# Reordering the first gate matmuls of a fused state-space and feed-forward kernel: four tiles first, then two double-width tiles, with the fourth token tile loaded earlier

## Chip, cores, metric

The kernel runs on one core of a Trainium2 chip. The metric is the time of one execution in device microseconds (us). "Before" is the kernel without the change, "after" the kernel with it. All runs told here were with a granted TensorE clock of 0.999 or 1.0 of full speed.

Engine names in the profile: PE is TensorE matmul, PEld its weight load, DVE is VectorE, ACT is ScalarE, POOL is GpSimd; SPq and ACTq are the two queues from which this kernel issues its loads. A load "lands" when its data have arrived; the trace records the landing of each load in shares, 16 for a load that fills 128 partitions. "Evicting" is copying a result out of PSUM, the memory into which TensorE writes; PSUM has banks, and this kernel evicts a bank before it uses it again.

## The reference, cut to what matters

```python
def reference(A_x, ...):                 # x is 1 x 2048 x 512
    xn = layernorm(x)                    # per token, over 512 features
    # A: diagonal complex state-space layer, 512 states, scanned over 2048 tokens
    # B: (silu(xn @ w_gate) * (xn @ w_up)) @ w_down, hidden width 1376
    return x + A(xn, ...) + B(xn, w_gate, w_up, w_down)
```

Everything needs `xn`, so nothing useful can run on TensorE before the first tokens are loaded, normalised and transposed. The change is about that start.

## The kernel before

The tokens come in four chunks of 512. TensorE does, for each chunk, gate, up and state-input matmuls, then one long accumulation of the down-projection and the state output. For chunk 0 the gate matmuls of the first six hidden tiles are cut into quarters of 128 tokens (`q`), so that they can start when one tile of 128 tokens is ready. Six PSUM banks stay open for them. In front of the gates PE also runs some matmuls on a constant whose result is not used (`pe_warm`, line 450).

The loads of the start, in the order of their queues (`dma` issues on SP, `act_load` on ACT):

```python
act_q = [pload("ld_ldt", 2, A_log_dt)]                       # a parameter row
dma("ld_x0", ...); dma("ld_x1", ...)                         # 128 tokens each, 128 KB
act_load("ld_wgA0", wg[:, 0:2, 0:FQ], ..., [("wg", "a0")])   # gate tiles 0-3, first half of the contraction
dma("ld_x2", ...)
act_load("ld_wgA1", wg[:, 2:4, 0:FQ], ..., [("wg", "a1")])   # gate tiles 0-3, second half
dma("ld_wg0", wg[:, :, FQ:FH0], ...)                         # gate tiles 4, 5
dma("ld_x3", ...)
act_q.append(pload("ld_lim", ...)); act_q.append(pload("ld_lre", ...))   # parameter rows
```

Normalisation of the first tiles (`bn_st`, `bn_ag` statistics, `ln_ve` variance plus epsilon, `ln_rstd` the power on POOL, `ln_apply` the result) and the gate loop:

```python
def ln_chunk0():
    bn_st(0); bn_ag(0)
    last = ln_ve(0, 1)
    ln_rstd(0, 1)
    last = ln_apply(0, parts=2, order=(bn_st(1, order=(last,)),))
    last = ln_ve(1, 1, order=(bn_ag(1, order=(last,)),))
    ln_rstd(1, 1)
    return bn_st(2, order=(last,))
# ... ln_chunk0_rest(): apply 1; then tiles 2 and 3, with the parameter copy params_ev between

xt_tile_fine(0, parts=2, ...)          # PE transposes of token tile 0, ACT evicts them into xnT
for q in range(4):                     # 128 tokens each
    for ii, (i, bk) in enumerate(tiles):   # six gate tiles
        if q == 0 and ii == 2:
            params_t(...)              # PE transposes the parameter rows
            ln_chunk0_rest(...)
        if q < 3 and ii == (4 if q == 0 else 2):
            xt_tile_fine(q + 1)        # transposes of the next token tile
        # 4 matmuls: wg[:, kt, i] (128 x 128) times xnT[:, 0, q, kt, :] (128 tokens)
```

PE and SP keep the program order written here. The order on DVE, ACT and POOL comes from a list scheduler in the kernel, which works with estimated times.

## Time and profile before

| | before |
|---|---|
| median (runs) at the time of the prediction | 181.9 us (3; 181.77 to 181.97) |
| profiled run | 182.01 us, span 180.3 us |
| PE busy | 97% of the span |
| first gate matmul | 6.76 us |
| first up-projection | 13.47 us |
| last output addition | 177.83 us |

First, two lines of the profile's page (the span, then busy us, share and number of instructions by engine).

```profile
span 180.3 us, 2342 instructions
...
PE 175.3 (97%) x900; PEld 84.9 (47%) x908; DVE 160.8 (89%) x274; ACT 84.5 (47%) x107; POOL 13.5 (7%) x23
...
```

The list of waits of PE (who waited for whom: us in total, times, longest).

```profile
...
PE pb L749 <- ACT xnT L549: 1.0, 2, 0.8
PE pb L450 <- PEq L977: 0.8, 1, 0.8
PE pb L543 <- DVE xn_sb L485: 0.2, 1, 0.2
```

PE waited for 2.0 us in all, always at the start. The chain of work that ended last, in order of time (start, its length in us, what), shows where the end is decided:

```profile
...
6.13 0.63 issue
6.76 0.61 PE pb L749 x8
...
13.63 13.81 PE pb L710 x64
...
177.83 0.42 DVE x_sb L881
```

From 13.63 us on the chain is PE work alone to within 0.05 us at each hand-over, up to the last output addition at 177.83. A gain must come from before 13.5 us, or the tail. The timeline of PE there (start, us, engine, line, operation, output<-inputs, form, count, idle before):

```profile
...
6.76 0.61 PE L749 MATMUL pb<-xnT,wg 128*128 128x128 bf16 x8 [0.75 <-ACT xnT L549]
7.30 0.22 PE L457 MATMUL pb<-ident,prow 4*128 4x4 bf16 x3
7.46 0.62 PE L749 MATMUL pb<-xnT,wg 128*128 128x128 bf16 x8
7.92 0.39 PE L543 MATMUL pb<-ident,xn_sb 128*128 128x128 bf16 x4
8.14 0.61 PE L749 MATMUL pb<-xnT,wg 128*128 128x128 bf16 x8
8.99 0.62 PE L749 MATMUL pb<-xnT,wg 128*128 128x128 bf16 x8 [0.24 <-ACT xnT L549]
...
13.47 0.81 PE L710 MATMUL pb<-xnT,wu 128*128 128x512 bf16 x3
```

How to read it: matmuls of 128 columns start 0.056 us apart but each record lasts 0.22 us, so a group's record ends later than its issue slots. The eight that begin at 8.14 have used their slots by 8.14 + 8 x 0.056 = 8.59. The next group begins at 8.99. The gap is 0.40 us of issue although the line says 0.24. The transposes of token tile 1 (7.92, line 543) are what it waits for: transposes, eviction by ACT and hand-over take 8.99 - 7.92 = 1.07 us.

In the second chain line, "issue" for 0.63 us before 6.76 hides a wait. The timeline names ACT for it, but by the chain ACT had evicted tile 0 by 6.13: the second half of the gate weights was issued at 1.83 us, and the trace's landing records have 15 of its 16 shares by 5.64 us and the last at 6.67. The Trainium skill ("DMA: Bandwidth & Descriptors", section "Why a DMA increments its semaphore by 16 and not by 1") says that only the full 16 means that all data landed. The trace agrees: the first gate matmul starts 0.09 us after the sixteenth.

### The profile page before, as it was taken

What the parts mean: (1) busy time and instruction counts of PE and PEld (TensorE: products, weight loads), DVE (VectorE), ACT (ScalarE), POOL (GpSimd) and SP (SyncE); (2) the same over time, 40 slices, a digit from 0 to 9 for tenths busy, and PEclk for the clock granted to TensorE, in tenths of its full rate; (3) what the DMA queues carried; (4) which work ended last, traced back from release to release, by engine and by line L of the source; (5) the groups of instructions that cost most, each with busy time, mean ns of one, the idle gap of its engine ahead of it and who ended that gap; (6) DMA issues with size and microseconds to landing.
All of it is one profiled execution on the core that took longest, in us unless ns stands there. A gap on an engine that the chain in (4) does not pass through costs nothing.

```text
span 180.3 us, 2342 instructions
## 1 busy us (share of the span) xinstructions
PE 175.3 (97%) x900; PEld 84.9 (47%) x908; DVE 160.8 (89%) x274; ACT 84.5 (47%) x107; POOL 13.5 (7%) x23
## 2 busy tenths in 40 slices
PE   8799999999999999999999999999999999999994
PEld 2494444444444444444444544444444444444643
DVE  3888849989799999979999999999999999999733
ACT  3279899995897991060655653000455620000000
POOL 3251200004200000320000000000000000000000
PEclk9999999999999999999999999999999999999999
DMA  6995556669160000001430000001200000000202
GB/s 163 316 373 127 119 100 104 149 201 343 33 116 0 4 0 0 0 0 61 91 86 0 0 0 4 0 0 36 80 0 4 0 0 0 0 0 33 87 29 87
DMA packets 23410, 12.37 MB, mean 69 GB/s; under 512 B 15112, under 2 KB 23400, under 8 KB 23400
## 3 DMA queue, kind: packets, MB, share of 16 engines
q1 hardware_dynamic: 22832, 11.70, 24.4%
q10 hardware_dynamic: 568, 0.53, 1.0%
q8 instruction: 7, 0.11, 0.3%
q14 instruction: 3, 0.02, 0.0%
HBM read 6.46 MB, written 2.10 MB: 47 GB/s over the span
## 4 chain that ended last, share of the span: by engine, by line
PE 94%; DMA 1%; DVE 1%; issue 1%; ACT 1%; POOL 0%
PE pb L710 39%; PE pb L863 21%; PE pb L781 15%; PE pb L876 15%; PE pb L749 3%; DMA x_sb<-in_A_x_dram 1%; ACT xnT L549 1%; PE pb L543 1%; DVE st L466 0%; POOL rstd L478 0%; DVE x_sb L881 0%; DVE xn_sb L485 0%; DVE mv L470 0%; DVE ve L474 0%; PE pb L457 0%
## 5 line engine op out<-in xcount | busy, mean ns | idle before, releaser
L710 PE MATMUL pb<-xnT,wu 128*128 128x512 bf16 (+1 forms) x176 | 41.2, 379 | 0.0
L821 DVE TENSOR_TENSOR_SCAN rot<-sm,car,rot 128x512 bf16<-128x512 f32 x32 | 38.9, 1267 | 0.0
L863 PE MATMUL pb<-wd,hT 128*128 128x512 bf16 (+3 forms) x183 | 38.0, 366 | 0.2
L710 PE MATMUL pb<-xnT,wg 128*128 128x512 bf16 (+1 forms) x152 | 35.9, 379 | 0.0
L722 ACT ACTIVATE sg<-pb 128x1024 bf16<-128x1024 f32 (+1 forms) x24 | 22.4, 948 | 28.4 <-PE pb L710 28.1
L876 PE MATMUL pb<-W,hss 128*128 128x512 bf16 (+1 forms) x132 | 28.1, 366 | 0.2
L781 PE MATMUL pb<-xnT,BT 128*128 128x512 bf16 x128 | 28.1, 379 | 0.0
L863 PEld LDWEIGHTS pb<-wd,hT 128*128 128x128 bf16 (+1 forms) x187 | 18.3, 98 | 20.0
L768 ACT ACTIVATE uf<-pb 128x1024 bf16<-128x1024 f32 (+1 forms) x24 | 22.7, 950 | 9.4 <-PE pb L710 8.6
L710 PEld LDWEIGHTS pb<-xnT,wu 128*128 128x128 bf16 (+1 forms) x176 | 17.6, 100 | 20.1
L710 PEld LDWEIGHTS pb<-xnT,wg 128*128 128x128 bf16 (+1 forms) x152 | 15.3, 100 | 17.6
L876 PEld LDWEIGHTS pb<-W,hss 128*128 128x128 bf16 x136 | 13.3, 98 | 14.4
L781 PEld LDWEIGHTS pb<-xnT,BT 128*128 128x128 bf16 x128 | 12.5, 98 | 15.0
L788 ACT ACTIVATE u_sb<-pb 128x1024 bf16<-128x1024 f32 x16 | 16.3, 1022 | 5.1 <-PE pb L781 4.8
L770 DVE TENSOR_TENSOR hT<-sg,uf 128x1024 bf16<-128x1024 bf16 (+1 forms) x24 | 14.9, 635 | 2.8 <-ACT uf L768 2.8
L881 DVE TENSOR_TENSOR x_sb<-pb,x_sb 128x512 bf16<-128x512 f32 (+1 forms) x17 | 10.9, 654 | 5.4 <-PE pb L876 5.4
L466 DVE BATCH_NORM_STATS2 st<-x_sb 128x6 f32<-128x512 bf16 x16 | 10.2, 682 | 4.0 <-DMA x_sb<-in_A_x_dram 4.0
L495 ACT ACTIVATE xn_sb<-x_sb,nmr,rstd 128x512 bf16<-128x512 bf16 x8 | 5.9, 802 | 10.5 <-DVE nmr L492 10.5
L812 DVE TENSOR_TENSOR rot<-u_sb,cosT 128x2048 bf16<-128x2048 bf16 x8 | 9.7, 1215 | 0.4 <-ACT u_sb L788 0.4
L812 DVE TENSOR_TENSOR rot<-rot,sin 128x2048 bf16<-128x2048 bf16 x8 | 9.8, 1220 | 0.0
L812 DVE TENSOR_TENSOR rot<-rot,cosT 128x2048 bf16<-128x2048 bf16 x8 | 9.8, 1220 | 0.0
L812 DVE TENSOR_TENSOR rot<-u_sb,sin 128x2048 bf16<-128x2048 bf16 x8 | 9.7, 1214 | 0.0
(62 smaller groups left out, 115.7 us busy)
## 6 DMA issues: line engine op xcount, KB each, us to landing
out_dram<-x_sb SPq DMA_DIRECT2D x15, 128.0 KB, 1.7
x_sb<-in_A_x_dram SPq DMA_DIRECT2D x3, 512.0 KB, 7.6
wd<-in_B_w_down_dram SPq DMA_DIRECT2D x1, 1280.0 KB, 7.0
wu<-in_B_w_up_dram SPq DMA_DIRECT2D x1, 768.0 KB, 6.4
wg<-in_B_w_gate_dram SPq DMA_DIRECT2D x1, 608.0 KB, 7.5
wu<-in_B_w_up_dram SPq DMA_DIRECT2D x1, 608.0 KB, 8.7
x_sb<-in_A_x_dram SPq DMA_DIRECT2D x4, 128.0 KB, 2.8
wg<-in_B_w_gate_dram ACTq DMA_DIRECT2D x2, 256.0 KB, 4.0
```

The lines of the kernel that those rows point to most:

```text
L466: return g.add("dve", lambda e, a=a: e.bn_stats(out=st[:, a, :], in_=x_sb[:, a, :]), reads=[("x", a)], writes=[("st", a)], name="bnst%d" % ...
L710: inst = e.matmul(pbank[0:fs, bk, :].rearrange("p (j t) -> p j t", j=4), lhsT=w[:, kt, i * 128:i * 128 + fs], rhs=xnT[:, c % 2, :, kt, :], ...
L722: g.add("act", lambda e: e.activation(out=sg[rows, sl, 0:n, :].rearrange("p a t -> p (a t)"), in_=pair_f32(rows, bk, 512 * n), func=AF.Sil ...
L768: g.add("act", lambda e: e.activation(out=uf[rows, ul, 0:n, :].rearrange("p a t -> p (a t)"), in_=pair_f32(rows, bk, 512 * n), func=AF.Ide ...
L770: g.add("dve", lambda e: e.tensor_tensor(out=hT[rows, hb, i0:i0 + n, :], in0=sg[rows, sl, 0:n, :], in1=uf[rows, ul, 0:n, :], op=ALU.mult), ...
L781: inst = e.matmul(pbank[:, bk, :].rearrange("p (j t) -> p j t", j=4), lhsT=BT[:, ri, kt, pt * 128:(pt + 1) * 128], rhs=xnT[:, c % 2, :, kt ...
L788: g.add("act", lambda e: e.activation(out=u_sb[:, us].rearrange("p r t -> p (r t)"), in_=pair_f32(slice(0, 128), b0), func=AF.Identity), r ...
L812: tt = lambda out, a, b, op, r, w, nm: g.add("dve", lambda e: e.tensor_tensor(out=out, in0=a, in1=b, op=op), reads=r, writes=w, name="%s_% ...
L821: g.add("dve", lambda e, A0=A0, A1=A1, k=k, ri=ri, pt=pt: e.tensor_tensor_scan(out=A1[:, k, ri, :], data0=rr[:, pt:pt + 1].to_broadcast([1 ...
L863: inst = e.matmul(pbank[:, bk, 0:nc_], lhsT=hT[0:fs, hb, i, lt * 128:(lt + 1) * 128], rhs=wd[0:fs, i, c0:c0 + nc_], start=(i == 0), stop=F ...
L876: inst = e.matmul(pbank[:, bk, 0:nc_], lhsT=hss[:, hb, pt, ri, lt * 128:(lt + 1) * 128], rhs=W12[:, ri, pt, c0:c0 + nc_], start=False, sto ...
L881: g.add("dve", lambda e, bk=bk, a=a, c0=c0, nc_=nc_: e.tensor_tensor(out=x_sb[:, a, c0:c0 + nc_], in0=pbank[:, bk, 0:nc_], in1=x_sb[:, a, ...
```

## The change

The intent: ask for fewer weights early, get the transposes of the second token tile out sooner, and have the tokens' statistics ready in time.

- PE: four gate tiles for tokens 0-127 and then for 128-255; the last two gate tiles later, for both at once (256 columns); transposes of token tile 1 after two gate tiles instead of four.
- Loads: x3 before the weights of gate tiles 4 and 5.
- DVE and POOL: the mean and variance of token tile 1 before tile 0 is applied; tile 1's `ve` on POOL; statistics of tile 3 before the parameter copy.

```diff
+        dma("ld_x3", x_sb[:, 3:4, :], x_v[:, 3:4, :], [("x", 3)], TILEB)
         dma("ld_wg0", wg[:, :, FQ:FH0], wg_v[:, :, FQ:FH0], [("wg", 0)], 512 * (FH0 - FQ) * 2)
-        dma("ld_x3", x_sb[:, 3:4, :], x_v[:, 3:4, :], [("x", 3)], TILEB)
@@ ln_chunk0
-            last = ln_apply(0, parts=2, order=(bn_st(1, order=(last,)),))
-            last = ln_ve(1, 1, order=(bn_ag(1, order=(last,)),))
+            last = bn_ag(1, order=(bn_st(1, order=(last,)),))
+            ln_ve(1, 1, eng="pool")
             ln_rstd(1, 1)
+            last = ln_apply(0, parts=2, order=(last,))
             return bn_st(2, order=(last,))
@@ ln_chunk0_rest
                 if a == 2:
-                    last = params_ev(par_bank, (last,))
-                last = ln_apply(a, order=(bn_st(a + 1, order=(last,)),) if a < 3 else (last,))
+                    last = params_ev(par_bank, (bn_st(3, order=(last,)),))
+                last = ln_apply(a, order=(last,))
@@ ffn_gate_quarters (the loop over q is replaced; gate() is four matmuls, cut here)
+            gate(i, bk, 0, 1, 0, 2, fine=True)      # tile, bank, first quarter, quarters
+            gate(i, bk, 0, 1, 2, 4, fine=True)
+            gate(*tiles[1], 0, 1)
+            params_t(tiles[-1][1])
+            ln_chunk0_rest(last, tiles[-1][1])
+            xt_tile_fine(1)
+            gate(*tiles[2], 0, 1)
+            gate(*tiles[3], 0, 1)
+            gate(*tiles[0], 1, 1)
+            gate(*tiles[1], 1, 1)
+            xt_tile_fine(2)
+            gate(*tiles[2], 1, 1)
+            gate(*tiles[3], 1, 1)
+            gate(*tiles[4], 0, 2)
+            gate(*tiles[5], 0, 2)
+            for ii, t in enumerate(tiles):
+                if ii == 2:
+                    xt_tile_fine(3)
+                gate(*t, 2, 1)
+            for t in tiles:
+                gate(*t, 3, 1)
```

More of the change, by code (lines that the diff above doesn't have):

```diff
@@ L738, in ffn_gate_quarters, with gate, mm @@
             tiles = [(2 * ip + k, banks[ip] + k) for ip in pairs for k in range(2)]
-            for q in range(4):
-                for ii, (i, bk) in enumerate(tiles):
-                    if q == 0 and ii == 2:
-                        params_t(tiles[-1][1])
-                        ln_chunk0_rest(last, tiles[-1][1])
-                    if q < 3 and ii == (4 if q == 0 else 2):
-                        xt_tile_fine(q + 1)
-                    for k0, k1 in (((0, 2), (2, 4)) if q == 0 and ii == 0 else ((0, 4),)):
-                        def mm(e, bk=bk, i=i, q=q, k0=k0, k1=k1):
-                            for kt in range(k0, k1):
-                                inst = e.matmul(pbank[:, bk, q * 128:(q + 1) * 128], lhsT=wg[:, kt, i * 128:(i + 1) * 128], rhs=xnT[:, 0, q, kt, :],
-                                                start=(kt == 0), stop=(kt == KT - 1))
-                            return inst
-                        xr = [("xnT", 0, q)] if q else [("xnT0", h) for h in range((k1 + 1) // 2)]
-                        g.add("pe", mm, reads=wres("wg", i) + xr, writes=BK(bk), name="mm_gq%d_%d" % (i, q), est=(k1 - k0) * 56, ninst=k1 - k0)
+            def gate(i, bk, q0, nq, k0=0, k1=KT, fine=False):
+                def mm(e):
+                    for kt in range(k0, k1):
+                        o = pbank[:, bk, q0 * 128:(q0 + nq) * 128]
+                        inst = e.matmul(o.rearrange("p (j t) -> p j t", j=nq), lhsT=wg[:, kt, i * 128:(i + 1) * 128], rhs=xnT[:, 0, q0:q0 + nq, kt, :],
+                                        start=(kt == 0), stop=(kt == KT - 1))
+                    return inst
+                xr = [("xnT0", h) for h in range((k1 + 1) // 2)] if fine else [("xnT", 0, q0 + j) for j in range(nq)]
+                g.add("pe", mm, reads=wres("wg", i) + xr, writes=BK(bk), name="mm_gq%d_%d" % (i, q0), est=(k1 - k0) * (56 if nq == 1 else 110), ninst=k1 - k0)
@@ new lines, in ffn_gate_quarters @@
+            (i, bk) = tiles[0]
+            gate(i, bk, 0, 1, 0, 2, fine=True)
[11 more added lines that the diff above has]
+            gate(*tiles[3], 1, 1)
```

## The prediction

> **What bounds the kernel now.** TensorE: the busy table gives PE 97% of the 180.3 us span at full granted clock. The chain of waits is PE work without a break from 13.63 us (first up-projection) to 177.8; the list of waits shows PE waiting three times, 0.8, 1.0 and 0.2 us in total, all before 9 us. VectorE is 89% busy but ahead: the last `hss` is ready at 165.9 us and first used at 170.7. So the change can gain only before 13.5 us.
>
> **The first 13.5 us, from the timeline.** Token tile 0 is normalised, transposed and evicted by 6.13 us. The first gate matmul starts at 6.76, and not for the normalisation: the second gate-weight half (ACT queue, issued 1.83) lands at 6.67. Its landing records show 15 of 16 shares by 5.64 us and one at 6.67. The Trainium skill ("DMA: Bandwidth & Descriptors", why a DMA increments its semaphore by 16) says that only all 16 mean landed; the trace agrees. The parameter rows, behind it on that queue, land at 7.06; their transposes start at 7.30. From 6.76 to 13.47 are 6.71 us: 96 gate matmuls x 0.056 = 5.35, 12 transposes x 0.055 = 0.66, parameters 0.16, and about 0.4 idle before 8.99, where PE waits for tile 1's eviction: its transposes start at 7.92, its gates can start 1.07 us later, and only 8 matmuls (0.45 us) stand between. After that no wait.
>
> **What the change does.**
> - PE order: tile 1's transposes come 0.46 us earlier, but its gates follow 8 matmuls behind, as before: 1.07 us against 0.22 + 0.45 of work. The idle of 0.4 us moves to about 8.1-8.5 us and stays. Later evictions remain covered.
> - Eight 256-wide matmuls replace sixteen 128-wide. The Trainium skill ("TensorE: Matmul & The Clock Gate", "Wait — 56ns, not 53.3ns?") gives N / 2.4 GHz plus about 2.5 ns; the trace agrees (56 ns at 128, 216 at 512). Estimate: 0.02 us gained.
> - VectorE: tile 1's mean goes first (tile 0 maybe 0.05 us later), its `ve` moves to POOL, tile 3's statistics precede the parameter copy. Tiles 1 to 3 are ready slightly earlier, but they are ready 0.6-1 us before PE asks, before and after. Off the critical path.
> - x3 (landed 7.57) goes ahead of the weights of gate tiles 4, 5, which are now asked for near 9.7 instead of 8.14; they landed at 7.25, so no wait there before either.
> - Scheduling: a sine table moves ahead of the SiLU evictions (0.65 us); banks have about 1.5 us of slack there.
>
> Sum: first gate start unchanged, gates end at 13.42 instead of 13.47: nominally -0.05 us.
>
> **What can move it.** The straggling weight share and the parameter rows: another DMA (128 packets rather than 512) is now issued just behind. If the straggler goes, gates start at 6.2 and the parameters near 6.7: up to 0.6 us gained. If the larger packets slow it, 0.2-0.3 lost.
>
> **Predicted time: 181.75 us, 80% range 181.3 to 182.15.** Faster by over 2%: 0.005; within 2%: 0.99; slower by over 2%: 0.005.
>
> **What would show it.** Right: first gate matmul at 6.2-6.9 us, at the weights' landing; one PE wait of about 0.4 us for tile 1's eviction, now before 8.5 us; first up-projection at 12.9-13.6 us; PE unbroken from there, so that the total moves by just that start. Wrong: a PE wait for tile 2, 3, gate tiles 4, 5 or a bank; the total moved without the first up-projection; a gap after 13.5 us.

## The result

| | before | after |
|---|---|---|
| median of 6 runs | 181.76 us (181.53 to 181.97) | 181.83 us (181.71 to 182.53) |
| ratio after / before | | 1.0011, 95% interval 0.9993 to 1.0028 |
| profiled run | 182.01 us | 182.53 us |
| second gate-weight half complete | 6.67 us | 6.61 us |
| first gate matmul | 6.76 us | 6.70 us |
| first up-projection | 13.47 us | 13.38 us |
| last output addition | 177.83 us | 178.34 us |

A ratio here is the mean time of one kernel's fast runs over that of the other's of the same rounds, so it is not quite the ratio of the medians in the table. The slowest run after, 182.53, is the one that was profiled; without it the ratio of the means would be 1.0005. The page after:

```profile
span 180.8 us, 2337 instructions
...
PE 175.8 (97%) x900; PEld 84.7 (47%) x900; DVE 160.4 (89%) x273; ACT 84.1 (47%) x107; POOL 14.0 (8%) x24
...
```

The list of waits of PE after, and its timeline of the start:

```profile
...
PE pb L450 <- PEq L995: 0.8, 1, 0.8
PE pb L544 <- DVE xn_sb L485: 0.6, 1, 0.6
PE pb L744 <- DMA wg<-in_B_w_gate_dram: 0.4, 1, 0.4
PE pb L711 <- ACT sg L723: 0.4, 1, 0.4
PE pb L744 <- ACT xnT L550: 0.2, 1, 0.2
```

```profile
...
6.70 0.61 PE L744 MATMUL pb<-xnT,wg 128*128 128x128 bf16 x8 [0.45 <-DMA wg<-in_B_w_gate_dram]
7.23 0.22 PE L457 MATMUL pb<-ident,prow 4*128 4x4 bf16 x3
7.39 0.40 PE L544 MATMUL pb<-ident,xn_sb 128*128 128x128 bf16 x4
7.62 0.61 PE L744 MATMUL pb<-xnT,wg 128*128 128x128 bf16 x8
8.47 0.62 PE L744 MATMUL pb<-xnT,wg 128*128 128x128 bf16 x8 [0.24 <-ACT xnT L550]
...
13.38 1.24 PE L711 MATMUL pb<-xnT,wu 128*128 128x512 bf16 x5
```

The start is as predicted, nearly figure by figure. The first gate matmul follows the landing of its weights, and now the profile names that DMA. Transposes of tile 1 begin 0.16 us after the parameter transposes (7.39 after 7.23) instead of 0.62 (7.92 after 7.30). But the gates that need them begin at 8.47, again 1.08 us later, and again only eight matmuls lie between: 7.62 + 8 x 0.056 = 8.07, so PE issues nothing for 0.40 us. The gap moved and kept its size. First gate matmul to first up-projection is 13.38 - 6.70 = 6.68 us, against 6.71 before.

One thing was not predicted: the fourth wait of the list, `PE pb L711 <- ACT sg L723`, far behind the start. The chain after has it:

```profile
...
1.81 4.80 DMA wg<-in_B_w_gate_dram
6.61 0.09 issue
6.70 0.61 PE pb L744 x8
...
13.54 13.81 PE pb L711 x64
...
51.00 0.92 ACT sg L723
...
178.34 0.42 DVE x_sb L899
```

The timeline at 48 to 53 us, before and then after:

```profile
...
49.35 1.00 ACT L722 ACTIVATE sg<-pb 128x1024 bf16<-128x1024 f32 x1
...
51.45 1.89 PE L710 MATMUL pb<-xnT,wg 128*128 128x512 bf16 x8
...
```

```profile
...
48.06 2.93 ACT L495 ACTIVATE xn_sb<-x_sb,nmr,rstd 128x512 bf16<-128x512 bf16 x4 [2.38 <-DVE nmr L492]
...
50.90 1.00 ACT L723 ACTIVATE sg<-pb 128x1024 bf16<-128x1024 f32 x1
...
51.96 1.25 PE L711 MATMUL pb<-xnT,wg 128*128 128x512 bf16 x5 [0.43 <-ACT sg L723]
...
```

In the run after, ACT began to normalise chunk 2 (line 495, four instructions) at 48.06, because its statistics waited for x tiles 8 to 11. The SiLU eviction (`sg`) stood behind in ACT's order, started 1.55 us later than before (50.90 against 49.35), and PE waited for its bank: 51.96 against 51.45, although PE had been 0.09 us ahead. That costs 0.6 us in this run. The landing records show a cause up the line: one share of the transposing load of `C_re` came at 34.38 us, 1.54 us after the fifteenth, and the DMAs behind it were issued later (x tiles 8 to 11 at 38.30 instead of 36.56 us). Was this part of the change, or an accident of one run? The repeat below decides.

### The profile page after: what moved, and what is told of

It reads as the page before. It is cut to its first block, busy times and chain, and to the rows that moved or that the text cites. A ratio compares the mean times of both kernels' runs of the same rounds, so it can differ in the third digit from the quotient of the medians.

```text
span 180.8 us, 2337 instructions
## 1 busy us (share of the span) xinstructions
PE 175.8 (97%) x900; PEld 84.7 (47%) x900; DVE 160.4 (89%) x273; ACT 84.1 (47%) x107; POOL 14.0 (8%) x24
## 4 chain that ended last, share of the span: by engine, by line
PE 94%; DMA 3%; ACT 1%; ACTq 1%; DVE 0%; issue 0%
PE pb L711 39%; PE pb L881 21%; PE pb L894 15%; PE pb L799 15%; PE pb L744 3%; DMA wg<-in_B_w_gate_dram 3%; ACTq L385 1%; ACT sg L723 1%; PE pb L544 0%; ACT xnT L550 0%; DVE x_sb L899 0%; PE pb L457 0%
## 5 line engine op out<-in xcount | busy, mean ns | idle before, releaser
L711 PE MATMUL pb<-xnT,wu 128*128 128x512 bf16 (+1 forms) x176 | 41.2, 379 | 0.0
L881 PE MATMUL pb<-wd,hT 128*128 128x512 bf16 (+3 forms) x187 | 38.7, 366 | 0.0
L711 PE MATMUL pb<-xnT,wg 128*128 128x512 bf16 (+1 forms) x152 | 35.9, 379 | 0.4 <-ACT sg L723 0.4
L723 ACT ACTIVATE sg<-pb 128x1024 bf16<-128x1024 f32 (+1 forms) x24 | 22.4, 949 | 26.7 <-PE pb L711 26.5
L711 PEld LDWEIGHTS pb<-xnT,wu 128*128 128x128 bf16 (+1 forms) x176 | 17.6, 100 | 20.1
L711 PEld LDWEIGHTS pb<-xnT,wg 128*128 128x128 bf16 (+1 forms) x152 | 15.2, 101 | 18.3 <-ACT sg L723 0.9
L894 PEld LDWEIGHTS pb<-W,hss 128*128 128x128 bf16 x136 | 13.3, 98 | 14.4
```

The source lines that it names most:

```text
L711: inst = e.matmul(pbank[0:fs, bk, :].rearrange("p (j t) -> p j t", j=4), lhsT=w[:, kt, i * 128:i * 128 + fs], rhs=xnT[:, c % 2, :, kt, :], ...
L723: g.add("act", lambda e: e.activation(out=sg[rows, sl, 0:n, :].rearrange("p a t -> p (a t)"), in_=pair_f32(rows, bk, 512 * n), func=AF.Sil ...
L881: inst = e.matmul(pbank[:, bk, 0:nc_], lhsT=hT[0:fs, hb, i, lt * 128:(lt + 1) * 128], rhs=wd[0:fs, i, c0:c0 + nc_], start=(i == 0), stop=F ...
L894: inst = e.matmul(pbank[:, bk, 0:nc_], lhsT=hss[:, hb, pt, ri, lt * 128:(lt + 1) * 128], rhs=W12[:, ri, pt, c0:c0 + nc_], start=False, sto ...
```

## The experiments

Twelve kernels were run, in four groups (e1 to p3, e2 to e5, f1 to f3, and f4 alone, in the order of the table); each group shared its chip and its runs of the kernel before. All were correct.

| kernel | median us (runs) | before in the same rounds | ratio, 95% interval |
|---|---|---|---|
| e1: the change again | 181.89 (5) | 181.85 (11) | 1.0004, 0.9993 to 1.0016 |
| p1: loads only | 181.77 (6) | 181.85 (11) | 0.9998, 0.9986 to 1.0011 |
| p2: normalisation only | 181.94 (5) | 181.85 (11) | 0.9999, 0.9986 to 1.0012 |
| p3: PE order only | 181.94 (5) | 181.85 (11) | 1.0001, 0.9989 to 1.0013 |
| e2: transposes early, six gate tiles | 181.68 (6) | 181.70 (11) | 1.0000, 0.9984 to 1.0017 |
| e3: weights issued first | 181.92 (6) | 181.70 (11) | 1.0012, 0.9997 to 1.0027 |
| e4: e2 and e3 | 181.81 (6) | 181.70 (11) | 1.0006, 0.9992 to 1.0021 |
| e5: e4 with the change's normalisation | 181.78 (6) | 181.70 (11) | 1.0004, 0.9988 to 1.0020 |
| f1: e2 with ACT order mended | 181.46 (6) | 181.85 (11) | 0.9992, 0.9967 to 1.0017 |
| f2: gate weights cut by columns | 182.26 (6) | 181.85 (11) | 1.0017, 0.9997 to 1.0038 |
| f3: f1, f2 and later parameters | 181.49 (6) | 181.85 (11) | 0.9981, 0.9963 to 0.9999 |
| f4: f1 with x 8-11 loaded earlier | 181.36 (6) | 181.75 (11) | 0.9980, 0.9962 to 0.9999 |

And what the profiled run of each shows of the start (us):

| kernel | second gate-weight load complete | first gate matmul | first up-projection | last output addition | profiled run |
|---|---|---|---|---|---|
| before | 6.67 | 6.76 | 13.47 | 177.83 | 182.01 |
| after | 6.61 | 6.70 | 13.38 | 178.34 | 182.53 |
| e1 | 6.45 | 6.54 | 13.36 | 177.72 | 181.89 |
| p1 | 6.09 | 6.18 | 12.95 | 177.31 | 181.48 |
| p2 | 6.82 | 6.95 | 13.66 | 178.01 | 182.18 |
| p3 | 6.80 | 6.89 | 13.58 | 177.94 | 182.12 |
| e2 | 6.44 | 6.53 | 13.39 | 177.75 | 181.95 |
| e3 | 5.88 | 6.45 | 13.34 | 177.69 | 181.87 |
| e4 | 5.34 | 6.55 | 13.42 | 177.78 | 181.94 |
| e5 | 5.23 | 6.68 | 13.06 | 177.41 | 181.59 |
| f1 | 6.09 | 6.39 | 12.74 | 177.10 | 181.29 |
| f2 | 6.97 | 5.93 | 13.55 | 177.91 | 182.09 |
| f3 | 7.00 | 6.00 | 12.83 | 177.19 | 181.36 |
| f4 | 6.04 | 6.13 | 12.52 | 176.88 | 181.06 |

Two readings of this table carry the rest. First, in 13 of the 14 profiles the last output addition comes 164.35 or 164.36 us after the first up-projection; only the run after, with its late wait, has 164.96. So apart from such an accident the total is the start plus a constant: the profiled run's time less its first up-projection is 168.52 to 168.56 us in those 13. Second, wherever the gate weights came last (before, after, p1, p2, p3, f4), the first gate matmul starts 0.09 to 0.13 us after their last share. In e1 and e2 it also starts 0.09 us after, but there the `pe_warm` matmuls in front of it on PE end within 0.02 us of the same moment, so these two cannot tell which was last. The weights' last share moved between 6.04 and 6.82 us over these profiles without a cause in the code that these runs show. The 44 timed runs of the kernel before in the four groups reach from 181.27 to 182.47 us. The start has one more part that moves. In e1, e2 and f1 the last `pe_warm` matmuls (256 columns) started 0.213 us apart, against 0.109 to 0.113 in before and after, and the trace's first record of the full TensorE clock is at 6.82, 6.61 and 6.50 us, against 4.49 and 4.18. In f1 the last of them started at 6.18 and the first gate matmul followed at 6.39, 0.30 us after the weights: PE's own work held it there. **One profile therefore cannot judge a change of half a microsecond here**: p1's profiled run is 0.5 us shorter than that of before, but its six timed runs give a ratio of 0.9998.

### e1: the change, again

No edit.

> The changed kernel unaltered, once more, to see which of its features repeat. Theory (start bound by the second gate-weight half, idle moved and not filled): ratio to the kernel before 0.998 to 1.002; first gate matmul within 0.1 us of the landing of that weight half; a PE wait of about 0.25 us in the list (0.4 us in issue) for tile 1's eviction before 9 us. The PE wait of 0.4 us near 51 us in the first profile of the changed kernel (ACT held by the late normalisation of chunk 2): the accident theory says that it came from one late share of a transpose of the C matrix and is absent or under 0.2 us here; the rival (the change's own order on VectorE and ACT makes it) says that it is here again with 0.4 us or more.

Measured: ratio 1.0004 and no wait of PE after the start:

```profile
...
PE pb L450 <- PEq L995: 0.8, 1, 0.8
PE pb L744 <- ACT xnT L550: 0.2, 1, 0.2
```

The gap is there again (8.46 after 7.61 + 0.45 = 8.06). The wait near 51 us is not, with the same order of instructions on every engine. So that order does not make it by itself. With the late load it did: 1.55 us of delay in the run after, where the kernel before has about 1.1 us to spare. The change's total was the start's in e1, as predicted. From first gate matmul to first up-projection e1 took 6.82 us, not 6.68: its first three steps from one gate matmul to the next took 0.094 to 0.106 us, until the clock record of 6.82, and the rest of the eight 0.055 to 0.057.

### p1, p2, p3: each part alone

p1 swaps the two loads alone, p2 takes the normalisation hunks alone, p3 the PE hunk alone, each on the kernel before, as in the diff of the change.

> The kernel before with only x3 loaded ahead of the weights of gate tiles 4 and 5. Theory: statistics of tile 3 start near 6.9 instead of 7.6 us, nothing on PE moves: first up-projection 13.3 to 13.6 us, ratio 0.998 to 1.002. In this order the weights of tiles 4 and 5 land near 7.9 us and PE asks for them near 8.1, so a wait of up to 0.2 us is possible. Rival (the loads are what the change is worth): ratio under 0.998.

> The kernel before with only the normalisation order of the change (tile 1 mean first, its variance on POOL, tile 3 statistics before the parameter copy). Theory: tile 1 is normalised about 0.1 us earlier, PE asks for it only near 7.9 us, so ratio 0.998 to 1.002 and the first up-projection at 13.3 to 13.6 us. Rival (it delays tile 0 and so the start): first gate matmul later by 0.1 to 0.25 us and ratio 1.001 or more.

> The kernel before with only the PE order of the change (transposes of tile 1 after two gate tiles; gate tiles 4 and 5 late and 256 wide). Theory: the PE gap before the gates of tokens 128-255 moves to about 8.1-8.5 us and stays 0.4 us in issue; first up-projection 13.3 to 13.5 us; ratio 0.998 to 1.002. Rival (the order does fill the gap and something else gives it back): gap under 0.15 us.

Measured: 0.9998, 0.9999 and 1.0001. No part is worth anything that these runs can show; the intervals leave room for 0.14%, or 0.25 us, so larger gains and losses that cancel are excluded. p3 has its tile 1 transposes at 7.59, its two gate tiles from 7.82 and the next gates at 8.68; 8.68 - (7.82 + 0.45) = 0.41 us, the moved gap:

```profile
...
7.82 0.61 PE L743 MATMUL pb<-xnT,wg 128*128 128x128 bf16 x8
8.68 0.62 PE L743 MATMUL pb<-xnT,wg 128*128 128x128 bf16 x8 [0.24 <-ACT xnT L549]
...
```

The rival of p3 (the order fills the gap) falls. In p1 and p2 the starts differ from before by more than the theory allows (first up-projections 12.95 and 13.66 against the 13.3 to 13.6 that I wrote), but by the landing of the second weight half, 6.09 and 6.82; from the first gate matmul to the first up-projection they take 6.77 and 6.71 us. p2's rival said that the start would be late because tile 0 is late; tile 0's transposes end early enough there (second group starts at 5.50), and PE's wait is for the weights.

### e2: fill the gap

On the kernel before:

```diff
-                    if q < 3 and ii == (4 if q == 0 else 2):
+                    if q < 3 and ii == 2:
```

> The kernel before with one edit: the transposes of tile 1 come after two gate tiles as in the change, but the gates of tokens 0-127 keep all six tiles, so 16 matmuls (0.9 us) and not 8 (0.45 us) stand between these transposes and the gates that need them. Theory (too little work behind the transposes is the gap): no PE gap before the gates of tokens 128-255, first up-projection at 13.0 to 13.15 us, ratio 0.9970 to 0.9985 (0.3 to 0.5 us). Rival (start-up gaps are not on the critical path, or something later gives it back): ratio 0.999 or more.

Measured: 1.0000, and 13.39 instead of 13.0 to 13.15. This expectation failed. PE's timeline and, in the second fence, ACT's:

```profile
...
7.55 1.50 PE L749 MATMUL pb<-xnT,wg 128*128 128x128 bf16 x24
...
10.68 1.06 PE L749 MATMUL pb<-xnT,wg 128*128 128x128 bf16 x16
12.04 1.51 PE L749 MATMUL pb<-xnT,wg 128*128 128x128 bf16 x24 [0.31 <-ACT xnT L549]
...
```

```profile
...
10.78 0.73 ACT L660 ACTIVATE scrC<-iot,sm 128x512 f32<-128x512 f32 x1 [0.87 <-DVE sm L612]
11.42 0.57 ACT L549 ACTIVATE xnT<-pb 128x512 bf16<-128x512 bf16 x1
...
```

The first gap is gone: 24 matmuls run without a break from 7.55. But a new gap opens at the last quarter: 10.68 + 16 x 0.056 = 11.58, and the next group begins at 12.04. ACT shows why. The eviction of token tile 3 (line 549) starts at 11.42, although its transposes were issued at 10.45; a sine-table activation (line 660) that was scheduled in front of it ran from 10.78. Before, PE was slower to get there, and the same order cost nothing. What the early transposes had won, 0.40 us, was given back as 0.46 us at the end of the same stage.

### e3, e4, e5: issue the weights earlier

e3, on the kernel before, puts the parameter row behind the weights on the ACT queue:

```diff
-        act_q = [pload("ld_ldt", 2, A_log_dt)]
+        act_q = []
...
         act_load("ld_wgA1", ...)
+        act_q.append(pload("ld_ldt", 2, A_log_dt, (act_q[-1],)))
```

(`act_load` takes `tuple(act_q[-1:])` as its order, since the list may now be empty.) e4 has the edits of e2 and e3, e5 adds the normalisation hunks of the change.

> The kernel before with one edit: on the ACT queue the two gate-weight halves are issued ahead of the parameter row ld_ldt, so about 0.56 us earlier. Theory (the first gate matmul waits for the second half): it starts at 6.15 to 6.35 us, now bound by tile 0's eviction; first up-projection at 12.95 to 13.2 us; ratio 0.9965 to 0.9985. Rival (the landing is set by shared DMA bandwidth or the straggling share and not by the issue): first gate matmul at 6.6 us or later and ratio 0.999 or more. If x0 lands later for it, up to 0.2 us of the gain goes.

> The edits of e2 and e3 together. Theory: gains add, first up-projection at 12.6 to 12.8 us, ratio 0.994 to 0.9965 (0.6 to 1.0 us). Less if tile 1 (normalised by about 6.7 us in the kernel before) or the weights of gate tiles 4 and 5 (landing 7.25) become what PE waits for: then a PE wait for one of them shows, and the gain is 0.4 to 0.6 us.

> e4 with the normalisation order of the change added. Theory: with the start 0.5 us earlier, tile 1's readiness has little slack left, so this order is worth 0 to 0.1 us now; ratio within 0.001 of that of e4. Rival (tile 0 is delayed by tile 1's mean, and tile 0's eviction now sets the start): 0.05 to 0.25 us slower than e4.

Measured: 1.0012, 1.0006 and 1.0004. No gain: e3 and e4 both missed their ranges, and e5 came within 0.001 of e4, as expected. The weights did land earlier (5.88, 5.34, 5.23), but no longer set the start. PE's first groups in e3 (transposes of tile 0, then the gates):

```profile
...
5.71 0.27 PE L544 MATMUL pb<-ident,xn_sb 128*128 128x128 bf16 x2 [0.46 <-DVE xn_sb L486]
...
6.45 0.79 PE L750 MATMUL pb<-xnT,wg 128*128 128x128 bf16 x8
...
```

x0 landed at 3.41 instead of 2.93 us, x1 at 4.46 instead of 3.67. Tile 0's transposes began at 5.71 instead of 5.14, and the gates at 6.45, now behind tile 0's eviction. In e3, e4 and e5 x0 landed at 3.29 to 3.41 us, in the other eleven profiles at 2.82 to 2.99: what the weights gained, the tokens lost. The Trainium skill ("DMA: Bandwidth & Descriptors", section "Queues, rings and completion order") says that SP and ACT each own one ring on each of the same 16 engines, and that an engine takes turns between its rings; these landings agree with it. My rival had the wrong form (the weights' landing does follow the issue). It was right on the ratio; the first gate matmul, at 6.45, lies between the 6.35 of the theory and the 6.6 of the rival.

In e4 the gates begin at 6.55, and the wait of e2 before the last quarter is back (0.35 us in issue, by the same arithmetic: 10.82 + 0.90 = 11.72 to 12.07), so the first up-projection is at 13.42 where I had expected 12.6 to 12.8. In e5 that wait is absent (tile 3's eviction starts at 11.05 us, in e4 at 11.44) and the first up-projection is at 13.06; its timed runs do not separate it from e4 (181.78 and 181.81 us). The runs of e3, e4 and e5 spread over 0.18 to 0.27 us each, against 1.06 us for the kernel before in the same rounds (6 runs each, against 11): a start that waits for the token loads was steadier in these runs than one that waits for the second weight half.

### f1: e2 with the order on ACT mended

On e2, the first table activation is ordered behind the eviction of tile 3:

```diff
-                g.add("act", evac, reads=BK(slot), ...)
+                hold["ev%d" % a] = g.add("act", evac, reads=BK(slot), ...)
@@ _tables
-                      ..., name="tm%d" % pt, est=620, prio=_CFG['prio_tab'])
+                      ..., name="tm%d" % pt, est=620, prio=_CFG['prio_tab'], order=(hold["ev3"],))
```

> e2 with one addition: the first activation that fills the sine tables is ordered behind the eviction of tile 3 on ACT. In e2 it sat in front, so that eviction started at 11.42 instead of about 10.9 us and PE waited 0.46 us (in issue) before the last 24 gate matmuls. Theory (e2's gap filling was real and was given back there): no PE wait between the first gate matmul and the first up-projection except a short one inside the first eight matmuls, first up-projection 6.2 to 6.45 us after the first gate matmul (6.71 in the kernel before, 6.86 in e2); ratio 0.9970 to 0.9988. Rival (start-up gaps do not reach the total): ratio 0.9992 or more although the gap is gone.

```profile
...
6.39 0.67 PE L749 MATMUL pb<-xnT,wg 128*128 128x128 bf16 x8
...
7.38 1.50 PE L749 MATMUL pb<-xnT,wg 128*128 128x128 bf16 x24
...
12.74 1.89 PE L710 MATMUL pb<-xnT,wu 128*128 128x512 bf16 x8
```

In the profile both gaps are gone: 12.74 - 6.39 = 6.35 us from the first gate matmul to the first up-projection (6.71 before, 6.68 after the change), and PE's list of waits has nothing but the wait at the program's begin. That is close to the 0.40 us of the gap; part of the start is hidden behind the slow `pe_warm` matmuls here, but f4, where the weights come last again, has 6.39. The timed runs are 181.29, 181.57, 181.35, 182.49, 181.34 and 182.21: four near 181.4, two far above. The ratio, 0.9992, misses the expected 0.9970 to 0.9988 and sits on the bound that I gave the rival, and its interval includes both theories: by time this run is inconclusive. The kernel before reached 182.47 us in the same rounds, so two such runs need not come from f1's edits.

### f2: cut the weight loads by columns

On the kernel before; the same bytes, but gate tiles 0 and 1 need only the first load:

```diff
-        act_load("ld_wgA0", wg[:, 0:2, 0:FQ], wg_v[:, 0:2, 0:FQ], ...)
+        act_load("ld_wgA0", wg[:, :, 0:256], wg_v[:, :, 0:256], ...)
-        act_load("ld_wgA1", wg[:, 2:4, 0:FQ], wg_v[:, 2:4, 0:FQ], ...)
+        act_load("ld_wgA1", wg[:, :, 256:FQ], wg_v[:, :, 256:FQ], ...)
-                return [("wg", "a0"), ("wg", "a1")]
+                return [("wg", "a%d" % (i // 2))]
```

> The kernel before with the two gate-weight loads of the ACT queue cut by columns (two gate tiles each, all of the contraction) instead of by contraction rows; same bytes, same issue order, 512 B rows instead of 1 KB. Theory: gate tiles 0 and 1 need only the first load (landing near 4.6 to 5.3 us), so the first gate matmul starts at tile 0's eviction, 6.1 to 6.35 us; but the parameter transposes, next in PE's order, wait for their rows, which land near 6.7 to 7.2 us, so PE idles there and the first up-projection gains 0 to 0.2 us: ratio 0.9985 to 1.0005. Rival (the parameter rows do not hold PE): ratio under 0.998.

```profile
...
5.93 0.78 PE L749 MATMUL pb<-xnT,wg 128*128 128x128 bf16 x8
7.40 0.21 PE L457 MATMUL pb<-ident,prow 4*128 4x4 bf16 x3 [0.69 <-DMA prow<-in_A_Lambda_re_dram]
...
```

The gates begin at 5.93, but PE then waits 0.7 us for the last parameter row, which landed at 7.31, and the first up-projection is at 13.55. The ratio is 1.0017, a little above the range that I wrote. The wait was not removed, only handed to the next load in PE's order, and the gap of 0.40 us is still there behind it (8.22 + 0.45 = 8.67 to 9.07).

### f3: all of it

On the kernel before: the edits of f1 and f2, and

```diff
                     if q == 0 and ii == 2:
-                        params_t(tiles[-1][1])
-                        ln_chunk0_rest(last, tiles[-1][1])
+                        ln_chunk0_rest_a(last)               # tile 1; tile 2 complete
                     if q < 3 and ii == 2:
                         xt_tile_fine(q + 1)
+                    if q == 0 and ii == 4:
+                        params_t(tiles[-1][1])
+                        ln_chunk0_rest_b(hold["xn2"], tiles[-1][1])   # parameter copy, tile 3
```

> All together on the kernel before: column split of f2, transposes of tile 1 after two gate tiles with six gate tiles for tokens 0-127, ACT order of f1, parameter transposes after four gate tiles, tile 2 normalised before the parameter copy and before tile 3's statistics. Theory: first gate matmul 6.1 to 6.4 us, first up-projection 12.4 to 12.8 us, PE unbroken after it, ratio 0.9950 to 0.9975. If the weights of gate tiles 4 and 5 (7.3 to 7.6 us) or tile 3's statistics (x3 at 7.6 us) come late, a PE wait of up to 0.3 us for them.

Measured: ratio 0.9981 (0.9963 to 0.9999), runs 181.36 to 181.65 us, first gate matmul at 6.00, first up-projection at 12.83 (a little above the expected 12.8). Two short waits remain. Tile 1's transposes begin at 6.70, 0.17 us after PE was free, because its normalisation ended at 6.64; gate tiles 2 and 3 begin at 7.05, 0.11 us late, just behind their weights (7.00). The parameter row (7.46) held nothing: its transposes start 0.15 us after the start of the last gate matmul in front of them, as they do before and after. The ratio is just above the expected 0.9950 to 0.9975: some 0.35 us (0.0019 x 181.85) where I had expected 0.45 to 0.9.

### f4: f1 with an earlier load of chunk 2

On f1, the load of x tiles 8 to 11 goes ahead of the two transposing C loads:

```diff
         def loads_stage_b2():
+            dma("ld_x8", x_sb[:, 8:12, :], ...)
             dma("ld_cre", CT[:, 0], A_C_re, ..., xpose=True)
             dma("ld_cim", CT[:, 1], A_C_im, ..., xpose=True)
-            dma("ld_x8", x_sb[:, 8:12, :], ...)
```

> f1 with the load of x tiles 8 to 11 moved ahead of the two transposing loads of the C matrices. In the profile of the changed kernel with the wait near 51 us, one share of a C transpose landed 1.6 us late, x 8 to 11 behind it, the normalisation of chunk 2 then held ACT in front of a SiLU eviction, and PE waited 0.6 us for the bank. Theory (the slow outliers of f1, 182.2 and 182.5 against 181.3 to 181.6 for the other four, are such late arrivals): without the transposes in front, statistics of chunk 2 start by 34 us instead of 40 us or later, and no run is more than 0.5 us above the fastest; median 181.1 to 181.6, ratio 0.9965 to 0.9985. Rival (the outliers come from the first 13 us): spread of 0.8 us or more here too.

```profile
...
PE pb L450 <- PEq L977: 0.8, 1, 0.8
```

```profile
...
6.13 0.70 PE L749 MATMUL pb<-xnT,wg 128*128 128x128 bf16 x8
...
12.52 2.11 PE L710 MATMUL pb<-xnT,wu 128*128 128x512 bf16 x9
```

Measured: median 181.36, ratio 0.9980 (0.9962 to 0.9999), statistics of chunk 2 from 31.43 us. From first gate matmul to first up-projection 6.39 us, and PE waits for nothing after that. The six runs spread over 0.57 us (181.06 to 181.63), just over the 0.5 that I wrote and under the rival's 0.8. Both f3 and f4 beat the kernel before in their own rounds by 0.2%, at the edge of what these rounds resolve, and as two of twelve comparisons. That f1's two slow runs were late chunk 2 loads is not shown: no profile caught one, and six runs without one is weak evidence.

## Why the prediction was right

- **What bounds the kernel, and where a gain can lie.** Right: the constant of 164.36 us from the first up-projection to the last addition, in 13 of 14 profiles, is PE without a break. The change reaches only what precedes it.
- **The first gate matmul waits for the last share of the second weight half.** Right, in six profiles (before and after among them) with a delay of 0.09 to 0.13 us; e1 and e2 cannot tell. f2, in which the first tiles no longer need that load, starts at 5.93.
- **The gap of 0.4 us moves and stays.** Right: 0.40 us before, 0.40 after, 0.40 in e1, 0.41 in p3. The count of matmuls between transposes and their first use was eight on both sides. Put sixteen there and the gap goes (e2, f1).
- **256-wide matmuls are worth 0.02 us.** Right, but too small to see in the total. The Trainium skill ("TensorE: Matmul & The Clock Gate", section "Wait — 56ns, not 53.3ns?") gives N / 2.4 GHz plus about 2.5 ns for each matmul. The trace agrees: in the run after, the eight of 256 columns start 0.109 us apart and take 0.874 us, where sixteen of 128 columns, 0.0558 us apart, take 0.893. First gate to first up-projection (6.71 before, 6.71 in p2, 6.68 after, 6.69 in p3) has the same sign, but e1's 6.82 shows how much else moves there.
- **Normalisation and loads are off the critical path.** Right: 0.9999 and 0.9998 alone. One size was off: the prediction allowed tile 0 a delay of 0.05 us, and in the run after its transposes began 0.24 us later (5.38, not 5.14), behind x1, which landed at 4.16 instead of 3.67. The weights came later still.
- **The total moves by the start of the first up-projection.** Right in e1, not in the first profile after, where the start moved by -0.09 us and the last addition by +0.51. A gap after 13.5 us was listed as a sign against the prediction. It appeared once, from a late load, and not in the repeat. The prediction had looked at bank slack near 14 us and not at the chain behind x tiles 8 to 11 near 50 us, where the kernel before has about 1.1 us (the bank was free at 50.35, PE took it at 51.45).
- **The straggling share may go or get worse.** Its size was about right: 6.04 to 6.82 us where it set the start. That x3 in front changes it is not shown: 6.61, 6.45, 6.09 with x3 in front, 6.67, 6.82, 6.80, 6.44, 6.04 without.

The predicted time was 181.75 us, the measured median 181.83. That they lie so close is partly luck: the prediction was made from 181.9 for the kernel before, whose median of 6 then came to 181.76, so the small gain that it reckoned with was not seen (ratio 1.0011).

What stays open: why the last share of a load comes late in some runs. In the run after, a 16 KB instruction-queue packet was in flight from 32.3 to 33.3 us, while `C_re` was loading; that is a coincidence in time and no more.

## What to carry to other kernels

A wait of PE for its own transposed input is as long as transposes, eviction and hand-over, less the PE work placed behind the transposes; to shrink it, raise that amount of work, since moving transposes and consumers together only moves the gap. When a start is set by several arrivals that lie within half a microsecond (tokens, weights, parameter rows, PE's own earlier work, and an evicting engine that is busy with something else), removing one hands the time to the next, so list the second and third arrival before estimating a gain. And where the rest of the program is one unbroken chain, compare the moment at which it begins over several runs, since one profile carries the lateness of one DMA share and the moment at which the clock was granted.

## What the Trainium skill lacked or had wrong

- "DMA: Bandwidth & Descriptors" says that all 16 shares must land, but gives no figure for how far the last trails. Here: 15 of 16 by 5.64 us and the last at 6.67 (second weight half, before), and 32.84 against 34.38 us (`C_re` in the run after). Each time the last share trailed by over a microsecond (1.03 and 1.54).
- The same page says that the two issuing queues share the 16 engines, without a number for what one costs the other. Here: weights issued about 0.56 us earlier on ACT made x0 on SP land 0.48 us later (2.93 to 3.41) and x1 0.79 us later (3.67 to 4.46) in e3; e4 and e5 agree (x0 at 3.37 and 3.29).
- "Perfetto Trace Analysis" warns, in its opening note, that matmul busy time is a bad metric because matmuls are pipelined, but does not say how to correct an idle time. Here the recorded idle of 0.24 us was an issue gap of 0.40 us, since records of 0.22 us start 0.056 us apart.
